# Contiguous 16-row partitions, the inverse second stage and the skip inside the MLP loop, streamed constants, table halves in a pipeline, LayerNorm on two engines

## The chip, the cores and the metric

The kernel runs on one core of one Trainium2 chip. The metric is the device time of one execution in microseconds (us); lower is better. A time without more words is the median of several executions, with their lowest and highest value in brackets. The engines are PE (TensorE, matmul; PEld is its weight load), DVE (VectorE), ACT (ScalarE), POOL (GpSimd) and SP (the queue that issues the DMAs). Tiles whose names begin with `ps_`, `pk` or `ml_p` hold what PE wrote (PSUM); to evacuate one is to copy it out with ACT or DVE. The granted clock (PEclk) is the share of full speed that PE was given.

## The reference

One state-space layer (the kernel K is a sum over 128 complex exponentials per channel, applied by FFT as a long convolution), then a gated MLP, both behind a LayerNorm and with a residual. L is 2048, D is 640, N is 128, F is 1728, all in bf16.

```python
# cut: input generation, dtype helpers
def _A_ref(u, A_re, A_im, B_re, B_im, C_re, C_im, log_dt, Dskip):
    dt = jnp.exp(log_dt)[:, None]
    logdA = dt * A                                        # A, Bc, Cc complex, D x N
    P = jnp.exp(logdA[:, :, None] * l[None, None, :])      # l = 0..2047, as bf16
    K = jnp.einsum("dn,dnl,dn->dl", Cc, P, dt * Bc).real
    # ... Kf, Uf = rfft of K and u padded to 2 L
    y = irfft(Uf * Kf)[..., :L]
    return y + u * Dskip

def _B_ref(x, w_gate, w_up, w_down):
    return (sigmoid(x @ w_gate) * (x @ w_up)) @ w_down

h   = A_u + _A_ref(layernorm(A_u), ...)
out = h + _B_ref(layernorm(h), w_gate, w_up, w_down)
```

## The kernel before

The FFT is done as two stages of small DFT matmuls. The kernel K is made as a product of two tables of powers, A and B, that DVE builds by complex multiplications; 160 matmuls per half of the channels ("kernel matrix", `pk`) multiply them. `kv` is the diagonal part of that product in the layout that the spectrum needs. The channels are worked in two halves of 320, because the tables of one half fill the memory for tables. The parts that matter, in program order:

```python
def kmm(hf, kw):                                  # kernel matrix of one half
    for g0 in range(0, G, 6):
        # 12 matmuls into pk[:, i, :], then a strided cast on ACT
        nc.scalar.copy(kts[:, :, g0:g0 + n].rearrange("p x g -> p g x"), pk[:, 0:n, :])
    for m in range(4):
        for c in range(4):                        # 16 small DMAs move the diagonals
            sy.dma_start(kv[32*m:32*m+32, :, c*G:c*G+G], kts[c::4, 4*m+c:4*m+c+65:16, :])
    # ... and 5 for klast
def kspec(hf, kv, xu, ...):                       # spectrum of one half, 9 pairs
    for qp in range(9):
        # per q: load mk, 10 matmuls ps_xk, ACT: xk<-ps_xk
        # DVE: t1 = xu*xk, t2 = xu*swap(xk)
        # PE: inverse first stage ps_g from t1, t2;  ACT: g_stg<-ps_g;  DMA to d
        # ... cut
def is2(hf, g2, h, sd):                           # inverse second stage and skip, 16 rows
    for r in range(16):
        # us loaded from ud (u * Dskip, stored earlier); identity matmul of us
        # 4 matmuls of 32 columns with W4; DVE: h = ps_y + h
        # ... cut

# order
# LayerNorm statistics of 16 rows on DVE, bases, apply
u_s1()                                            # first stage -> d1u in DRAM
nc.vector.tensor_tensor(u[:], u[:], dsk, ALU.mult); sy.dma_start(ud[:], u[:])
chain_a(0); chain_b(0)                            # tables of half 0, DVE
u_s2(xu, W2, a2p)                                 # second stage, both halves
kv = kmm(0, kw)
bases(1); chain_a(1)
kspec(0, kv, ...)
chain_b(1)
kv = kmm(1, kw)
kspec(1, kv, ...)
is2(0, ...); is2(1, ...)
mlp(...)       # 4 row groups; LayerNorm of the next group after feature tile 6
# ... cut: allocations, constants, weight loads
```

Of the kernel before, what the change touches and what calls it, by code (L numbers as in the profile page):

```python
# [14 lines left out]
P = 128  # L15
D = 640
NSLOT = 72
# [8 lines left out]
A_STEPS = [(slice(3, 4), slice(1, 2), 2), (slice(5, 8), slice(1, 4), 4), (slice(9, 13), slice(1, 5), 8), (slice(13, 16), slice(5, 8), 8),  # L26
           (slice(17, 22), slice(1, 6), 16), (slice(22, 27), slice(6, 11), 16), (slice(27, 32), slice(11, 16), 16)]
# [3 lines left out]
NTS = 5  # L31


def host_consts():
    p = np.arange(128)
    j1 = p & 31
    F1 = np.zeros((128, 64))
    for col in range(64):
        F1[:, col] = np.cos(2 * np.pi * j1 * col / 64) if col < 33 else -np.sin(2 * np.pi * j1 * (col - 32) / 64)
    ri, j2 = p >> 6, p & 63  # L40
    k1 = np.arange(33)[:, None]
    k2 = np.arange(64)[None, :]
    phi = 2 * np.pi * j2[:, None, None] * (k1 + 64 * k2)[None] / 4096
    W2re = np.where(ri[:, None, None] == 0, np.cos(phi), np.sin(phi))
    W2im = np.where(ri[:, None, None] == 0, -np.sin(phi), np.cos(phi))
    q = np.arange(17)[None, :, None]
    l2 = np.arange(64)[None, None, :]
    psi = 2 * np.pi * l2 * (2 * q + ri[:, None, None] + 64 * j2[:, None, None]) / 4096
    W3a = np.concatenate([np.cos(psi), np.sin(psi)], axis=2)
    W3b = np.concatenate([-np.sin(psi), np.cos(psi)], axis=2)  # L50
    row = p & 63
    k1r = np.where(row < 33, row, row - 32)
    w = np.where((row == 0) | (row == 32), 1.0, 2.0)
    l1 = np.arange(32)[None, :]
    W4b = np.where(row[:, None] < 33, np.cos(2 * np.pi * k1r[:, None] * l1 / 64), -np.sin(2 * np.pi * k1r[:, None] * l1 / 64)) * w[:, None] / 4096
    W4 = np.zeros((128, 2, 32))
    for hh in range(2):
        W4[64 * hh:64 * hh + 64, hh] = W4b[64 * hh:64 * hh + 64]
    sel = np.zeros((128, 4, 32))
    for i in range(4):  # L60
        sel[0:i + 1, i, 31] = 1.0
    lr = np.arange(2048).astype(np.float32).astype(ml_dtypes.bfloat16).astype(np.int64)
    f = np.arange(34)[:, None] + 64 * np.arange(64)[None, :]
    E = np.exp(-2j * np.pi * (np.arange(2048)[:, None] * f.reshape(1, -1) % 4096) / 4096)
    S = np.zeros((2049, f.size), np.complex128)
    np.add.at(S, lr, E)
    S = S.reshape(2049, 34, 64)
    S[:, 33] = 0
    M = np.zeros((17, 128, 2, 5, 128))
    a = np.arange(32)  # L70
    for m in range(4):
        for j in range(5):
            blk = S[B_VAL[4 * j + m] + 8 * a]
            blk = blk.reshape(32, 17, 128).transpose(1, 0, 2)
            M[:, 32 * m:32 * m + 32, 0, j] = blk.real
            M[:, 32 * m:32 * m + 32, 1, j] = blk.imag
    return {"ident": np.eye(128), "F1": F1, "W2": np.stack([W2re, W2im], axis=1).reshape(128, -1),
            "W3": np.stack([W3a, -W3a, W3b], axis=1).reshape(128, -1), "W4": W4.reshape(128, -1), "sel": sel.reshape(128, -1),
            "M": M.reshape(17, 128, 1280)}


def Lview(dram2d):
    return dram2d.rearrange("(l1 q r) d -> q l1 r d", l1=32, q=4, r=16)
# [21 lines left out]
def full_kernel(tc, ins, out):  # L105
# [5 lines left out]
    xv, ov = Lview(x2d), Lview(o2d)  # L111
# [3 lines left out]
    d1u = dram.tile([64, NSLOT, D], BF16, name="d1u")  # L115
    ud = dram.tile([P, 16, D], BF16, name="ud")
    d2 = [dram.tile([64, 64, w], BF16, name=f"d2_{i}") for i, (_, w) in enumerate(HALVES)]
# [5 lines left out]
    stp = sc.pool("s1stg", bufs=3)  # L123
# [18 lines left out]
    for rg in range(4):  # L142
        for q in range(4):
            sy.dma_start(u[32 * q:32 * q + 32, 4 * rg:4 * rg + 4, :], xv[q][:, 4 * rg:4 * rg + 4, :])
# [4 lines left out]
    dsk = early.tile([P, D], BF16, name="dsk")  # L149
    sy.dma_start(dsk[:], ins["A_Dskip"].rearrange("(o d) -> o d", o=1).to_broadcast((P, D)))  # L150
    F1 = cload(cp, "F1", [P, 64])
    W4 = cload(cp, "W4", [P, 2, 32])
    sel = cload(cp, "sel", [P, 4, 32])
# [19 lines left out]
    phi = par.tile([P, D], I32, name="phi")  # L173
    nc.vector.tensor_scalar(phi[:], rr[:], 2.0 ** 32, None, ALU.mult)
# [6 lines left out]

    mv = early.tile([P, 16, 2], F32, name="mv")
    rstd = early.tile([P, 16], F32, name="rstd")
    nmr = early.tile([P, 16], F32, name="nmr")
    st = early.tile([P, 16, 2, 6], F32, name="ln_st")

    def ln_stats(st, mv, src, r):
        for hh in range(2):
            nc.vector.bn_stats(st[:, r, hh, :], src[:, r, 320 * hh:320 * hh + 320])  # L189
        nc.vector.bn_aggr(mv[:, r, :], st[:, r, :, :].rearrange("p a b -> p (a b)"))  # L190

# [6 lines left out]
    mhalf = cp.tile([P, 16], F32, name="mhalf")  # L198
    nc.gpsimd.memset(mhalf[:], -0.5)

    def ln_apply(dst, src, r, c):
        nc.vector.tensor_scalar(dst, src, rstd[:, c:c + 1], nmr[:, c:c + 1], ALU.mult, ALU.add)  # L202

    for r in range(16):
        ln_stats(st, mv, u, r)


    CB = par.tile([P, 2, D], BF16, name="CB")
# [12 lines left out]
    g.tensor_tensor(CB[:, 0, :], c1[:], c2[:], ALU.subtract)  # L221
    g.tensor_tensor(cr[:], cr[:], dbi[:], ALU.mult)
    g.tensor_tensor(ci[:], ci[:], dbr[:], ALU.mult)
    g.tensor_tensor(CB[:, 1, :], cr[:], ci[:], ALU.add)
# [6 lines left out]

    def base_group(hf, ks, i0):
        o, w = HALVES[hf]
        n = len(ks)
        ph = btmp.tile([P, 3, WM], I32, name="b_ph")
        for i, k in enumerate(ks):
            if k:
                nc.vector.tensor_single_scalar(ph[:, i, 0:w], phi[:, o:o + w], k, ALU.logical_shift_left)
            else:
                nc.vector.tensor_copy(ph[:, i, 0:w], phi[:, o:o + w])  # L240
        ab = btmp.tile([P, 3, WM], F32, name="b_ab")
        nc.scalar.activation(ab[:, 0:n, 0:w], ph[:, 0:n, 0:w], AF.Abs)
        sn = btmp.tile([P, 3, WM], BF16, name="b_sn")
        nc.scalar.activation(sn[:, 0:n, 0:w], ph[:, 0:n, 0:w], AF.Sin, scale=SIN_SCALE)
        cs = btmp.tile([P, 3, WM], BF16, name="b_cs")
        nc.scalar.activation(cs[:, 0:n, 0:w], ab[:, 0:n, 0:w], AF.Sin, scale=-SIN_SCALE, bias=hpi[:, 0:1])
        return sn, cs
# [4 lines left out]
    def open_tables(hf):  # L252
# [3 lines left out]
        T["M"] = tabp.tile([P, 2, 6, w], BF16, name="tabM")  # L256

    def bases(hf):
        o, w = HALVES[hf]
        A, B, M, e = T["A"], T["B"], T["M"], E[hf]  # L260
        nc.gpsimd.memset(A[:, 0, 0, :], 1.0)
        nc.gpsimd.memset(A[:, 1, 0, :], 0.0)
        for gi, (i0, n) in enumerate(((0, 3), (3, 2), (5, 3), (8, 3))):
            ks = exps[i0:i0 + n]
            sn, cs = base_group(hf, ks, i0)
            if i0 < 5:
                for i in range(n):
                    j = A_BASE[i0 + i][0]
                    nc.vector.tensor_tensor(A[:, 0, j, :], e[:, i0 + i, :], cs[:, i, 0:w], ALU.mult)  # L269
                    nc.vector.scalar_tensor_tensor(A[:, 1, j, :], e[:, i0 + i, :], -1.0, sn[:, i, 0:w], ALU.mult, ALU.mult)  # L270
            else:
                m0 = i0 - 5
                nc.vector.tensor_tensor(M[:, 0, m0:m0 + n, :], e[:, i0:i0 + n, :], cs[:, 0:n, 0:w], ALU.mult)
                nc.vector.tensor_tensor(M[:, 1, m0:m0 + n, :], e[:, i0:i0 + n, :], sn[:, 0:n, 0:w], ALU.mult)
        nc.vector.tensor_copy(B[:, :, 0, :], CB[:, :, o:o + w])

# [10 lines left out]
    def chain_a(hf):  # L287
        for dst, src, mi in A_STEPS:
            cmul(T["A"], dst, src, T["A"], mi, HALVES[hf][1])

    def chain_b(hf):
        for dst, src, mi in B_STEPS:
            cmul(T["B"], dst, src, T["M"], mi, HALVES[hf][1])


    def u_s1():
        k = 0
        for lp in range(8):
            stg = stp.tile([P, 4, D], BF16, name="s1_stg")
            for (o, w) in HALVES:  # L300
                for qp in range(2):
                    ps = ps2.tile([P, 2, 512], F32, name="ps_s1", tag="p2")
                    for c in range(2):
                        for qi in range(2):
                            q = 2 * qp + qi
                            nc.tensor.matmul(ps[64 * c:64 * c + 64, qi, 0:w], lhsT=F1[32 * q:32 * q + 32, :],  # L306
                                             rhs=u[32 * q:32 * q + 32, 2 * lp + c, o:o + w], start=True, stop=True,
                                             tile_position=(32 * q, 64 * c))
                    nc.scalar.copy(stg[:, 2 * qp:2 * qp + 2, o:o + w], ps[:, :, 0:w])
            for c in range(2):  # L310
                j0 = 2 * lp + c
                rows = d1u[j0:j0 + 49:16, :, :]
# [316 lines left out]
```

## Time and profile before

626.74 us in three runs at first (625.21 to 627.21), 625.98 (622.04 to 627.21) with the fourth. The profiled execution has a span of 623.8 us.

| engine | busy us | share of span |
|---|---|---|
| PE | 408.8 | 66% |
| DVE | 278.8 | 45% |
| ACT | 218.8 | 35% |

No engine bounds the whole. First, the page of the kernel before, its part 2: each digit is the busy share, in tenths, of one of 40 slices (15.6 us each).

```profile
...
PE   1000520347781367899345567386999999999997
...
DVE  5797999300009998420012123757622322332331
...
DMA  9500522597301144431269996934001001001001
...
```

PE is little used in the first eight slices (125 us) while DVE is full for most of them, PE is full at the end (the last 12 digits, the MLP), and in between the engines take turns. The turns are read from windows. This is the busy time of each engine in stretches of the kernel before; the columns are named in the second line, and a number in brackets is a count of instructions.

```profile
...
core 0: us, PE busy (x) PEld busy (x) DVE busy (x) ACT busy (x) POOL busy (x), PEclk, DMA share, GB/s
76.00:114.00 38.00, 10.51 (x76) 5.51 (x75) 35.64 (x50) 13.22 (x20) 0.00 (x0) 1.00 0.27 73
114.00:131.00 17.00, 0.06 (x1) 0.00 (x0) 2.90 (x1) 0.00 (x0) 0.63 (x1) 1.00 0.77 278
...
317.00:387.00 70.00, 46.35 (x303) 26.23 (x303) 14.20 (x28) 22.23 (x33) 0.00 (x0) 0.85 0.89 241
428.00:619.00 191.00, 190.99 (x1074) 91.81 (x1073) 63.51 (x114) 38.81 (x64) 3.77 (x6) 1.00 0.06 15
...
```

DVE works 35.64 of the 38 us before 114; then everything waits while data travel (PE 0.06 of 17 us); the spectrum of half 1 takes 70 us for 46.35 us of PE at a DMA share of 0.89; the MLP is PE alone, at a granted clock of 1.00.

The waits between are in the PE timeline of the kernel before. The columns are start, duration, what ran, and in brackets how long PE had been idle and for what it waited.

```profile
...
63.88 0.83 PE L306 MATMUL ps_s_351<-u,c_F_114 32*64 32x320 bf16 x4 [37.54 <-DVE u L202]
...
109.25 1.70 PE L360 MATMUL pk<-tabB,tabA 128*128 128x84 bf16 x9 [14.21 <-DVE tabB L284]
110.88 0.48 PE L306 MATMUL ps_s_572<-u,c_F_114 32*64 32x320 bf16 x4
111.29 2.77 PE L360 MATMUL pk<-tabB,tabA 128*128 128x84 bf16 x15
131.49 0.45 PE L340 MATMUL ps_s_671<-a2g,c_W_665 128*64 128x320 bf16 x1 [17.44 <-DMA a2g<-d1u]
...
199.94 5.11 PE L385 MATMUL ps_xk<-kv,mk 128*128 128x320 bf16 x20 [14.39 <-DMA klast_d<-kts]
...
317.05 3.36 PE L385 MATMUL ps_xk<-kv,mk 128*128 128x320 bf16 x12 [14.39 <-DMA klast_d<-kts]
```

The first-stage matmuls start at 63.9 us. At 109 us the tables of half 0 are done and 24 matmuls of the kernel matrix run; the trace has them ahead of the second stage, although the text of the program has them after it. The last four matmuls of the first stage (`ps_s_572`) stand behind nine of them and so come only at 110.9 us, 16 us after the four before them (94.56). Then PE stands before the second stage and waits 17.44 us for the first stage's data to come back from DRAM. That is not transit alone: the skip product, which waits for these four (DVE, 111.4 us, 5.49 us long), its store (issued at 116.9) and the load of W2 (124.6) come first, and the first loads of a2g are issued from 125.1 on. Twice, ahead of each half's spectrum, PE waits 14.39 us for the small transfers of kv and klast.

### The profile page before, as it was taken

How to read it: one execution, taken by the hardware profiler on the slowest of the kernel's cores; microseconds unless marked ns; L12 is line 12 of the kernel's file. 1: busy time of each engine (PE TensorE's matmuls, PEld its weight loads, DVE VectorE, ACT ScalarE, POOL GpSimd, SP SyncE). 2: the span in 40 equal slices, each digit the busy share in tenths (PEclk: the TensorE clock that was granted, in tenths of full speed). 3: DMA queues.
4: the chain of work that ended last, by engine and by line, in shares of the span. 5: the costliest groups of instructions: out<-in, count | busy, mean ns of one | idle time of the engine just before them, and what ended most of it. 6: DMA issues, size and time to landing. Idle time of an engine off the chain costs nothing.

```text
span 623.8 us, 6408 instructions
## 1 busy us (share of the span) xinstructions
PE 408.8 (66%) x2470; PEld 223.2 (36%) x2470; DVE 278.8 (45%) x492; ACT 218.8 (35%) x280; POOL 25.3 (4%) x30
## 2 busy tenths in 40 slices
PE   1000520347781367899345567386999999999997
PEld 1000100224671134667323344123444444444443
DVE  5797999300009998420012123757622322332331
ACT  5630661048994033477522333002311310310210
POOL 0342000000000000000000000002000000000000
PEclk9999999995655687786577888757999999999999
DMA  9500522597301144431269996934001001001001
GB/s 184 138 0 0 164 56 76 211 243 163 108 1 28 42 123 114 115 89 46 57 141 243 245 296 183 203 82 142 1 2 42 1 1 42 1 1 42 2 1 42
DMA packets 44638, 57.26 MB, mean 92 GB/s; under 512 B 13496, under 2 KB 37568, under 8 KB 43840
## 3 DMA queue, kind: packets, MB, share of 16 engines
q1 hardware_dynamic: 44608, 56.86, 34.6%
q8 instruction: 19, 0.31, 0.2%
q14 instruction: 11, 0.09, 0.0%
HBM read 40.29 MB, written 15.73 MB: 90 GB/s over the span
## 4 chain that ended last, share of the span: by engine, by line
PE 40%; DMA 4%; DVE 2%; SPq 2%; issue 1%; ACT 1%; POOL 0%; DVEq 0%; POOLq 0%
PE ml_po L562 10%; PE ml_pg L550 10%; PE ml_pu L550 10%; PE ps_xk L385 5%; DMA us<-ud 3%; SPq L365 2%; PE ps_g L401 1%; PE ps_y L421 1%; PE ps_y L424 1%; DMA mk<-s4c_M 1%; ACT xk L386 1%; PE ml_pt L537 1%; DVE ln_2779 L533 0%; PE ps_y L427 0%; DVE ln_st L189 0%
## 5 line engine op out<-in xcount | busy, mean ns | idle before, releaser
L385 PE MATMUL ps_xk<-kv,mk 128*128 128x320 bf16 x340 | 66.0, 362 | 37.3 <-DMA klast_d<-kts 28.8
L552 ACT ACTIVATE ml_sg<-ml_pg 128x512 bf16<-128x512 f32 (+1 forms) x56 | 33.4, 597 | 130.6 <-PE ml_pg L550 129.1
L360 PE MATMUL pk<-tabB,tabA 128*128 128x84 bf16 x320 | 58.5, 352 | 21.8 <-DVE tabB L284 15.8
L550 PE MATMUL ml_pu<-lnT,Wu 128*128 128x512 bf16 (+1 forms) x280 | 70.8, 381 | 0.0
L553 DVE TENSOR_TENSOR ml_hm<-ml_pu,ml_sg 128x512 bf16<-128x512 f32 (+1 forms) x56 | 38.6, 690 | 70.7 <-PE ml_pu L550 67.8
L550 PE MATMUL ml_pg<-lnT,Wg 128*128 128x512 bf16 (+1 forms) x280 | 69.6, 380 | 0.0
L562 PE MATMUL ml_po<-Wd,ml_hm 128*128 128x512 bf16 x448 | 64.5, 300 | 0.0
L385 PEld LDWEIGHTS <-mk 128*128 128x128 bf16 x340 | 37.8, 116 | 65.8 <-DMA klast_d<-kts 29.4
L361 ACT CAST kts<-pk 128x504 bf16<-128x504 f32 (+1 forms) x28 | 59.3, 2236 | 6.0 <-PE pk L360 5.5
L360 PEld LDWEIGHTS <-tabA 128*128 128x128 bf16 x320 | 50.9, 161 | 28.6 <-issue 25.1
L386 ACT CAST xk<-ps_xk 128x640 bf16<-128x640 f32 x34 | 23.5, 693 | 62.2 <-PE ps_xk L385 37.5
L562 PEld LDWEIGHTS <-ml_hm 128*128 128x128 bf16 x448 | 33.1, 97 | 31.7 <-issue 9.0
L550 PEld LDWEIGHTS <-Wg 128*128 128x128 bf16 (+1 forms) x280 | 27.1, 99 | 33.3 <-issue 2.8
L405 ACT CAST g_stg<-ps_g 128x640 bf16<-128x640 f32 (+1 forms) x34 | 22.5, 689 | 47.1 <-PE ps_g L401 38.7
L550 PEld LDWEIGHTS <-Wu 128*128 128x128 bf16 (+1 forms) x280 | 27.4, 99 | 31.3 <-issue 0.3
L564 DVE TENSOR_TENSOR ml_out<-ml_po,h 128x640 bf16<-128x640 f32 x16 | 13.2, 825 | 51.3 <-PE ml_po L562 51.3
L401 PEld LDWEIGHTS <-c_W_906 64*128 64x128 bf16 x264 | 16.0, 107 | 50.0 <-issue 45.3
L269 DVE TENSOR_TENSOR tabA<-e_146,b_cs 128x320 bf16<-128x320 bf16 x5 | 1.5, 322 | 68.9 <-PE pk L360 68.8
L306 PEld LDWEIGHTS <-c_F_114 32*64 32x64 bf16 x128 | 4.5, 123 | 64.6 <-issue 64.6
L306 PE MATMUL ps_s_351<-u,c_F_114 32*64 32x320 bf16 x4 | 0.8, 444 | 37.5 <-DVE u L202 37.5
L340 PEld LDWEIGHTS <-c_W_665 128*64 128x64 bf16 x132 | 10.7, 145 | 31.6 <-issue 26.8
L428 DVE TENSOR_TENSOR h<-ps_y,h 128x320 bf16<-128x320 f32 x32 | 15.6, 491 | 12.2 <-PE ps_y L424 7.5
(303 smaller groups left out, 482.7 us busy)
## 6 DMA issues: line engine op xcount, KB each, us to landing
mk<-s4c_M SPq DMA_DIRECT2D x34, 320.0 KB, 3.5
d1u<-s_stg SPq DMA_DIRECT2D x32, 160.0 KB, 2.6
a2g<-d1u SPq DMA_DIRECT2D x15, 320.0 KB, 6.1
u<-in_A_u_dram SPq DMA_DIRECT2D x16, 160.0 KB, 6.1
ud<-u SPq DMA_DIRECT2D x1, 2560.0 KB
h<-in_A_u_dram SPq DMA_DIRECT2D x4, 640.0 KB, 7.3
g_0_1957<-d_0_59 SPq DMA_DIRECT2D x2, 1280.0 KB
us<-ud SPq DMA_DIRECT2D x16, 160.0 KB, 3.4
```

Source lines behind the costliest of these rows:

```text
L360: nc.tensor.matmul(pk[:, i, :], lhsT=Av[ri][:, :, g0 + i], rhs=Bv[ri][:, :, g0 + i], start=(ri == 0), stop=(ri == 1))
L361: nc.scalar.copy(kts[:, :, g0:g0 + n].rearrange("p x g -> p g x"), pk[:, 0:n, :])
L385: nc.tensor.matmul(ps[:, ri, 0:w], lhsT=mk[:, ri, j, :], rhs=kv[:, j, :], start=(j == 0), stop=(j == 4))
L386: nc.scalar.copy(xk[:, qi, :, :], ps[:, :, 0:w])
L401: nc.tensor.matmul(ps[:, kpar, 0:w], lhsT=W3[sl, wi, q, :], rhs=t[sl, qi, ro, :], start=(i == 0), stop=(i == 3), tile_position=(64 * kpar, 0))
L405: nc.scalar.copy(stg[:, 2 * (q % 2):2 * (q % 2) + nk, :], ps[:, 0:nk, 0:w])
L428: nc.vector.tensor_tensor(h[:, r, o:o + w], ps[:, 0, 0:w], h[:, r, o:o + w], ALU.add)
L550: nc.tensor.matmul(ps[0:fw, :], lhsT=W[:, dc, f0:f0 + fw], rhs=rhs, start=(dc == 0), stop=(dc == 4))
L552: nc.scalar.activation(sg[0:fw, :], pg[0:fw, :], AF.Sigmoid)
L553: nc.vector.tensor_tensor(hm[0:fw, ft, :], pu[0:fw, :], sg[0:fw, :], ALU.mult)
L562: nc.tensor.matmul(po[:, c0:c0 + w], lhsT=hm[0:fw, ft, 128 * lr:128 * lr + 128], rhs=Wd[0:fw, ft, c0:c0 + w], start=(ft == 0), stop=(ft == ...
L564: nc.vector.tensor_tensor(ob[:, lr, :], po[:], h[:, l2r, :], ALU.add)
```

## The change

The intent: put 16 consecutive rows on a partition (longer contiguous transfers, full 128-row DFT matmuls, half the inverse matmuls); work the second stage by halves, so that half 0's runs beside the table chain; stream W2 and W3 in groups instead of keeping them; take kv out with matmuls (`pick`) instead of small DMAs; run the spectrum as a software pipeline, one pair behind; do the statistics of 8 of 16 rows on ACT; and do the inverse second stage and the skip of 12 of the 16 rows inside the MLP's loop. The diff, cut to its core:

```diff
-    for r in range(16):
+    for r in range(NDV):                              # 8 rows on DVE, 8 on ACT
         ln_stats(st, mv, u, r)
...
-        for m in range(4):
-            for c in range(4):
-                sy.dma_start(kv[32 * m:32 * m + 32, :, ...], kts[c::4, 4 * m + c:4 * m + c + 65:16, :])
+                for m in range(4):
+                    nc.tensor.matmul(pv, lhsT=pick[:, c, m, :], rhs=kts[:, 4 * m + c:4 * m + c + 65:16, :], ...)
+                nc.scalar.copy(kvv[:, :, c, g1:g1 + GC], pv)
...
+        prev = None
+        for qp in range(9):
+            cur = front(qp)                           # mk matmuls, xk, products
+            if prev is not None:
+                back(*prev)                           # inverse matmuls of the pair before
+            prev = cur
+        back(*prev)
...
-    nc.vector.tensor_tensor(u[:], u[:], bc(dsk[:, None, :], (P, 16, D)), ALU.mult)
-    sy.dma_start(ud[:], u[:])
     chain_a(0)
-    chain_b(0)
-    u_s2(xu, W2, a2p)
-    kv = kmm(0, kw)
-    bases(1)
+    bases(1, "A")
+    u_s2(0, xu, a2p, nc.scalar.copy)
+    chain_b(0)
+    bases(1, "B")
+    kv = kmm(0, ktp, kx)
+    u_s2(1, xu, a2p, nc.vector.tensor_copy)
+    seeds(1)
     chain_a(1)
...
-    is2(0, g2[0], h, sd)
-    is2(1, g2[1], h, sd)
...
-            if rc < 3 and ft == 6:
-                prep(rc + 1)
+            if rc < 3 and ft == 4:
+                prep(rc + 1, nxt)                     # now with the inverse stage of 4 rows
+                if rc < 2:
+                    nxt = tail_loads(rc + 2)          # loads h and g2, makes the skip product
# ... cut: layouts, constants, allocations
```

## The prediction

> **What bounds it now.** No single engine: PE is busy 66% of 623.8 us, DVE 45%, ACT 35%. Timeline and per-window busy times give a chain of stages:
> - 0-114: DVE, almost without pause (36 of 38 us in 76-114). LN stats are spread through the table chains, so first-stage matmuls start only at 63.9. GpSimd makes it worse: while it works at 25-38 us a 128x320 DVE op takes 1.65 us instead of 0.32. The Trainium skill ("GPSIMD Engine Reference", Specifications) says the two share SBUF interfaces; the trace agrees.
> - 114-157: PE waits 17.4 us for the round trip of the first-stage spectrum, then the second stage at DMA pace (227 GB/s, DMA share 1.02).
> - 157-203: kmm half 0 (30 us; strided ACT cast 2.24 us, PE 0.18 us a matmul), then 14.4 us of PE idle while small kv DMAs are issued.
> - 203-317: half 1's tables (DVE) beside spectrum of half 0, kmm half 1, 14.4 us idle for kv again.
> - 317-387: spectrum half 1, 70 us for 46 us of PE: DMA share 0.89, mk waits, and a 1.64 us PE wait for DVE per pair.
> - 387-429: inverse second stage, 11 us PE idle for skip data; LN.
> - 429-620: MLP, PE 190 of 191 us at clock 1.0.
>
> **What the change does, costed.**
> 1. Half of LN stats (8 x 0.95 us) leave DVE for ACT; against it half 1's bases come early (4 us). Summing DVE durations in the new order: chain B(0) ends at about 102 (was 109), first stage at about 80 (was 112), so second stage of half 0 runs beside chain B. kmm(0) starts about 104 instead of 157: the largest gain.
> 2. kv by pick matmuls: removes 14.4 us idle twice, adds 80 small matmuls per half (7-13 us, estimate from 0.1-0.19 us each). kmm about 43 us: ends 147 (was 203).
> 3. Second stage of half 1 comes after, evacuated by DVE (17 x 0.74 us): 16 us given back. Then DVE must do both chains of half 1 plus products, 72 us by sum from 147. kmm(1) starts about 229, ends about 272 (kv ready was 317).
> 4. Spectrum half 1: PE work falls (half the inverse matmuls, software pipelining) to 34 us, but mk, W3, weights and stores are about 12.8 MB; at 250 GB/s about 50 us, DMA-bound. Ends about 322 (was 387).
> 5. Only four rows' inverse stage stays before the MLP, which starts about 347 (was 429): g_1 round trip, then rows 4-7's h and g2 loads queue behind Wd and block in-order DVE and PE.
> 6. MLP grows: 12 rows x 6 matmuls (10 us), and three DVE bursts of about 13 us (PSUM adds, stats, LN, skip) against 9-10 us of PE work behind them: 8 us of stalls. MLP 210 us (was 191).
>
> Sum: 347 + 210 + 4, plus 2 for profile against timing: **563 us**, range 537 to 590. Faster 0.97, same 0.02, slower 0.01.
>
> **What would show it.** Windows: first kmm matmul near 104, first spectrum product near 175, first spectrum-1 matmul near 272 without kv DMA wait; DMA share over 0.9 in spectrum half 1; first gate matmul near 347; three PE gaps of 2-4 us near ps_y in the MLP; 1.6 us DVE ops during GpSimd work still there.
>
> **What would make it wrong.** 640-byte runs of the split a2g loads slower than 5 KB runs; PE clock staying low (0.53 in kmm before), making kmm and spectrum PE-bound; spectrum half 1 less DMA-bound (upside 12 us); bursts stalling the MLP more, or the MLP losing its clock of 1.0, which alone would cost tens of us.

## The result, and the profile after

557.17 us (556.89 to 558.31, 4 runs) against 625.98. The ratio is 0.8914, 95% interval 0.8871 to 0.8957. A ratio is the mean time of one kernel's fast runs over that of the other's of the same rounds, so it is not quite the ratio of the medians. Executions over 1.5% slower than the fastest of the same kernel are left out of the means. The changed kernel is faster by about 11%.

The page of the changed kernel, part 2 (40 slices of 13.9 us), lines that answer to those of before and the clock:

```profile
...
PE   1201734789655885699968359799979999999997
...
DVE  4899899400589999200653275732273236322321
...
PEclk9999998555557898555799669799988999999999
DMA  7330546500253477001798991200100010001001
...
```

DVE is now full for most of the first half. The exception is the kernel matrix of half 0: from 114.2 to 143.2 us DVE is busy for 1.6 of 29 us, since the tables of half 1 take the memory of half 0's, which are still being read; ACT (26.5 us busy) and PE (26.8 us, at a granted clock of 0.50) set the pace there. The MLP (the last 16 digits of PE) is no longer all nines in its clock. Busy time in stretches of the changed kernel, columns as before:

```profile
...
100.00:146.00 46.00, 40.89 (x260) 32.88 (x260) 6.95 (x26) 41.75 (x46) 0.67 (x2) 0.50 0.12 32
...
266.00:309.00 43.00, 34.02 (x236) 20.25 (x235) 23.42 (x45) 20.31 (x32) 0.00 (x0) 0.92 0.88 277
334.00:552.00 218.00, 207.81 (x1125) 99.97 (x1146) 86.65 (x163) 38.70 (x64) 3.94 (x6) 0.97 0.06 20
...
```

The first is the kernel matrix of half 0, the second the spectrum of half 1, the last the MLP, which became longer: 217.5 us from its first up matmul to the end of its last down matmul, against 191.2 before. Lines of the PE timeline of the changed kernel up to the MLP:

```profile
...
85.62 0.74 PE L352 MATMUL ps_s_562<-a2g,W2g 128*64 128x320 bf16 x4 [7.93 <-DMA a2g<-d1u]
...
100.30 1.71 PE L377 MATMUL pk<-tabB,tabA 128*128 128x84 bf16 x9 [0.43 <-DVE tabB L312]
...
```

```profile
...
225.78 3.59 PE L377 MATMUL pk<-tabB,tabA 128*128 128x84 bf16 x20 [5.92 <-DVE tabB L312]
...
301.45 2.89 PE L417 MATMUL ps_xk<-kv,mk 128*128 128x320 bf16 x20 [2.36 <-DMA mk<-s4c_M]
...
320.18 1.23 PE L474 MATMUL ps_y<-g_1_2551,c_W_101 128*128 128x320 bf16 x4 [6.11 <-DMA g_1_2551<-d_1_59]
...
334.32 0.56 PE L605 MATMUL ml_pu<-lnT,Wu 128*128 128x512 bf16 x1 [0.22 <-issue]
...
```

The kernel matrix of half 0 starts at 100.3 us, amid the second stage. No wait for klast is left. The spectrum of half 1 waits for mk. Then the last result of half 1 goes to DRAM and back (6.11 us of PE) and the MLP starts at 334.3. Inside the MLP there are new gaps:

```profile
...
350.19 2.88 PE L619 MATMUL ml_po<-Wd,ml_hm 128*128 128x512 bf16 x19
355.59 1.46 PE L590 MATMUL ml_pt<-c_ident,ln_2845 128*128 128x128 bf16 x8 [2.52 <-DVE ln_2845 L586]
...
359.53 4.62 PE L605 MATMUL ml_pg<-lnT,Wg 128*128 128x512 bf16 x15
...
365.07 1.24 PE L605 MATMUL ml_pg<-lnT,Wg 128*128 128x512 bf16 x5
...
```

PE waits 2.52 us for DVE's LayerNorm, the eight transposes after it take 1.46 us, and then 15 gate matmuls take 4.62 us, where groups of 5 take 1.24 us a little later.

Where the time went, from the two traces (us from the start):

| point | before | after | gained so far |
|---|---|---|---|
| first matmul of kernel matrix, half 0 | 109.3 | 100.3 | 9 |
| kernel matrix, half 0, done (last cast) | 187.9 | 146.1 | 42 |
| kernel matrix, half 1, starts | 255.0 | 225.8 | 29 |
| spectrum of half 1 starts | 317.1 | 266.1 | 51 |
| spectrum of half 1 ends | 386 | 309 | 77 |
| first up matmul of the MLP | 428.1 | 334.3 | 94 |
| end | 623.8 | 555.7 | 68 |

The gain isn't steady: 13 us of it are lost between the first two kernel matrices, and 26 us in the MLP. The experiments look for what each part of the change is worth, above all of the parts where the gain shrinks.

### The profile page after: what moved, and what is told of

Same layout as the page of the kernel before. It is cut to its first block, busy times and chain, and to the rows that moved or that the text cites. A ratio compares the mean times of both kernels' runs of the same rounds, so it can differ in the third digit from the quotient of the medians.

```text
span 555.7 us, 6282 instructions
## 1 busy us (share of the span) xinstructions
PE 412.9 (74%) x2417; PEld 233.8 (42%) x2440; DVE 294.1 (53%) x518; ACT 234.1 (42%) x341; POOL 26.4 (5%) x35
## 4 chain that ended last, share of the span: by engine, by line
PE 49%; DVE 27%; ACT 9%; DMA 9%; issue 2%; POOL 2%; SPq 1%; POOLq 0%; DVEq 0%; ACTq 0%
PE ml_pg L605 11%; PE ml_po L619 10%; PE ml_pu L605 10%; PE pk L377 7%; DVE tS L310 5%; ACT kts L378 5%; PE ps_xk L417 4%; DMA mk<-s4c_M 4%; DVE ln_st L216 3%; DVE tabB L311 3%; DVE u L235 2%; PE ps_kv L385 2%; DMA W2g<-s4c_W 2%; DVE tabB L312 2%; DVE h L478 2%
## 5 line engine op out<-in xcount | busy, mean ns | idle before, releaser
L378 ACT CAST kts<-pk 128x420 bf16<-128x420 f32 x32 | 62.8, 2081 | 9.8 <-PE pk L377 9.3
L619 PE MATMUL ml_po<-Wd,ml_hm 128*128 128x512 bf16 (+3 forms) x438 | 64.8, 298 | 0.6 <-issue 0.2
L417 PE MATMUL ps_xk<-kv,mk 128*128 128x320 bf16 x340 | 57.2, 328 | 10.0 <-DMA mk<-s4c_M 8.9
L389 DVE TENSOR_TENSOR klast<-ps_kv,uhead 4x20 bf16<-4x20 f32 x32 | 4.8, 166 | 65.4 <-ACT kv L387 65.4
L591 ACT COPY lnT<-ml_pt 128x512 bf16<-128x512 bf16 x8 | 4.7, 586 | 61.6 <-PE ml_pt L590 61.6
L332 PEld LDWEIGHTS <-c_F_99 128*128 128x128 bf16 x64 | 8.0, 126 | 51.7 <-issue 47.5
L449 ACT CAST g_stg<-ps_g 128x640 bf16<-128x640 f32 x32 | 21.0, 699 | 10.1 <-PE ps_g L445 7.5
L352 PEld LDWEIGHTS <-W2g 128*64 128x64 bf16 x136 | 10.0, 156 | 33.4 <-DMA W2g<-s4c_W 20.1
L478 DVE TENSOR_TENSOR h<-ps_y,h 128x640 bf16<-128x640 f32 x16 | 12.8, 819 | 13.9 <-PE ps_y L474 12.7
L310 DVE TENSOR_TENSOR tS<-tabA,tabMA 128x3200 bf16<-128x3200 bf16 (+3 forms) x14 | 19.5, 1393 | 0.7 <-ACT tabA L302 0.4
```

Of the source, the lines that this page charges most:

```text
L310: nc.vector.tensor_tensor(t, X[:, :, src, :], mm, ALU.mult)
L417: nc.tensor.matmul(ps[:, ri, 0:w], lhsT=mk[:, ri, j, :], rhs=kv[:, j, :], start=(j == 0), stop=(j == 4))
L449: nc.scalar.copy(stg[0][:, 2 * (q % 2):2 * (q % 2) + 2, :], ps[:, :, 0:w])
L478: nc.vector.tensor_tensor(hv, ps[:, :, 0:w], hv, ALU.add)
L619: nc.tensor.matmul(po[:, c0:c0 + w], lhsT=hm[0:fw, ft, 128 * lr:128 * lr + 128], rhs=Wd[0:fw, ft, c0:c0 + w], start=(ft == 0), stop=(ft == ...
```

## The experiments

Names with e change one thing in the changed kernel, names with b one thing in the kernel before, and c are combinations. Each ran with runs of the kernel before on its chip. The ratio to compare with is 0.8914 for experiments e and c, and 1 for b. The intervals of the ratios are half to three quarters of a per cent to each side, so where a difference is smaller than one per cent the times alone don't settle it, and the trace's points are given as well. All kernels gave correct results.

### b3: order alone, in the kernel before

```diff
-    u_s2(xu, W2, a2p)
-    kv = kmm(0, kw)
+    kts = kmm(0, kw)
+    u_s2(xu, W2, a2p)
+    kv = kvmove(0, kts, kw)      # the small DMAs of kv
```

> The kernel before with one change of order: the 160 kernel-matrix matmuls of half 0 come ahead of the second stage on PE, and the small kv transfers come after it; nothing else of the change. Theory (order alone gives most of the gain: PE waited 17.4 us for the spectrum's round trip while the tables were ready, and the tables of half 1 wait for half 0's kernel matrix to free their buffers): kernel matrix of half 0 from about 114 to 146, second stage to about 168, the table chain of half 1 and with it kernel matrix of half 1 start 30 to 40 us earlier (about 215 to 225 instead of 255), total 586 to 597 against 623 to 627. Rival (PE and DMA do the same work in series whatever the order; only the 17 us of waiting are filled): total 606 to 612.

Measured: 607.11 us (605.92 to 608.77) against 624.95, ratio 0.9718 (0.9679 to 0.9758). From the PE timeline of b3:

```profile
...
127.28 4.35 PE L360 MATMUL pk<-tabB,tabA 128*128 128x84 bf16 x24 [14.03 <-ACT kts L361]
...
195.60 4.26 PE L390 MATMUL ps_xk<-kv,mk 128*128 128x320 bf16 x20 [13.99 <-DMA mk<-s4c_M]
...
```

And from its ACT timeline:

```profile
...
124.97 8.95 ACT L361 CAST kts<-pk 128x504 bf16<-128x504 f32 x4 [13.68 <-DMA ud<-u]
...
```

The rival's number came true, but not its reason. The kernel matrix of half 0 runs from 108.5 to 153 us with a wait of 14.03 us in it: the first cast into kts waits 13.68 us until the store of the skip (`ud<-u`) has landed, since kts lies in the memory that u leaves. The second stage takes until 181, the kv transfers aren't hidden (13.99 us before 195.6), and the spectrum of half 0 starts 4 us earlier than before; the theory, with the second stage over at about 168, had it some 30 us earlier. The kernel matrix of half 1 starts at 219 instead of 255, as the theory had it, but with half 0's spectrum unfinished; the two share PE until 282, where before it was done at 302. So this order alone gives 18 of the 68 us. With the skip's store gone as well it should give more; that pair was not run and is left open.

### b1: the skip made again instead of stored and loaded, in the kernel before

```diff
-    nc.vector.tensor_tensor(u[:], u[:], bc(dsk...), ALU.mult)
-    sy.dma_start(ud[:], u[:])
 # in is2
-                sy.dma_start(us[:], ud[:, r:r + 2, o:o + w])
+                for i in range(2):
+                    nc.vector.tensor_scalar(us[:, i, :], h[:, r + i, o:o + w], rstd..., nmr..., ALU.mult, ALU.add)
+                    nc.vector.tensor_tensor(us[:, i, :], us[:, i, :], dsk[:, o:o + w], ALU.mult)
```

> The kernel before with the skip product made again from h in the inverse stage instead of stored after the first stage and loaded again. Theory (the skip's store stands ahead of the second stage's loads in the queue and its product ahead of them on DVE, and the inverse stage waits 11 us for its reload): second stage starts about 119 instead of 131.5, the inverse stage of half 0 has no 11 us wait, total 18 to 26 us less (600 to 607). Rival (the DVE product and store are hidden behind the spectrum's own store and load, and the recomputation, 64 DVE operations of 0.2 to 0.3 us, paces the inverse stage instead): less than 10 us gained, 614 to 624.

Measured: 619.79 us (616.31 to 623.84) against 624.95, ratio 0.9922 (0.9864 to 0.9979). From the PE timeline of b1, ahead of the second stage and in the inverse stage:

```profile
...
125.10 5.14 PE L340 MATMUL ps_s<-a2g,c_W 128*64 128x320 bf16 x32 [11.46 <-DMA a2g<-d1u]
```

```profile
...
410.80 0.45 PE L423 MATMUL ps_y<-us,c_ident 128*128 128x320 bf16 x1 [0.83 <-DVE us L421]
...
```

The rival held. The wait for the spectrum's round trip is 11.46 us instead of 17.44, so the skip's product and store had cost 6 us, not 12; the rest is the round trip itself. Those 6 to 8 us stay up to the end of half 1's spectrum, and then DVE, which makes the skip row by row, paces the inverse stage. The first up matmul of the MLP is at 428.6, where before it was at 428.1. The profiled run was also the slowest of the four, so how much of the 0.8% is real is open.

### e1: LayerNorm statistics back on DVE

```diff
-    ln_stats_act(slice(NDV, 16))
+    for r in range(NDV, 16):
+        ln_stats(st, mv, u, r)
```

> The changed kernel with the LayerNorm statistics of rows 8 to 15 put back on DVE (8 times 0.95 us as the trace of before has it). Theory (DVE paces the stretch to kmm half 0): the chain of tables of half 0 ends 7 to 8 us later (108 instead of 100.5 us), first kmm matmul near 108, total 563 to 565 us against 557.2. Rival (the statistics on ACT delay ACT's evacuation of the first stage by as much as they spare DVE): chain and total within 2 us of the changed kernel, 555 to 559.

Measured: 556.34 us (555.53 to 559.01), ratio 0.8947 (0.8883 to 0.9012): not told apart from the changed kernel. My theory fell. The PE timeline of e1:

```profile
...
91.32 1.28 PE L352 MATMUL ps_s<-a2g,W2g 128*64 128x320 bf16 x8 [1.40 <-DMA W2g<-s4c_W]
103.24 3.57 PE L377 MATMUL pk<-tabB,tabA 128*128 128x84 bf16 x20 [10.64 <-DVE tabB L312]
...
```

The table chain of half 0 ends only 2.9 us later (103.2 against 100.3), and the second stage of half 0 is over at 92.6 instead of 106.4: without the statistics ACT evacuates the first stage sooner, so the second stage begins at 74.0 instead of 85.6. So the rival's total came true, and in part its reason. The kernel matrix then runs without second-stage matmuls between, and its last matmul starts at 139.9 in both traces. Why only 2.9 us and not 7.6? The DVE timeline of the changed kernel shows what the statistics made room for:

```profile
...
23.59 8.75 DVE L235 TENSOR_SCALAR u<-u,rstd,nmr 128x640 bf16<-128x640 bf16 x8
...
63.13 2.94 DVE L235 TENSOR_SCALAR u<-u,rstd,nmr 128x640 bf16<-128x640 bf16 x8
...
```

Eight LayerNorm applies take 8.75 us beside GpSimd's work, and 2.94 us after it. In e1 the statistics stand there instead, at 0.42 us for half a row as elsewhere, and the applies come later, at 0.37 us. This agrees with the Trainium skill, "GPSIMD Engine Reference", Specifications, which says that GpSimd's contention is with DVE instructions in a 2-port mode or with two SBUF inputs: the applies were slowed here and the statistics not, and a product with two inputs in SBUF that ran beside GpSimd in e1 took 1.05 and 1.75 us instead of 0.65. Whether the applies use the 2-port mode no run here shows.

### e4: no GpSimd in the early part

```diff
-    g = nc.gpsimd
+    g = nc.vector            # C and B products; f_*, c1, c2 in bf16 instead of fp32
```

> The changed kernel with the C and B products of the early part done by DVE in bf16, nothing by GpSimd there. Theory (GpSimd slows DVE while it works): a 128x320 DVE op that took 1.65 us beside GpSimd takes 0.3 to 0.4 us, the first u apply x8 falls from 8.75 to about 3 us, DVE gets about 3.4 us of products to do, the chain of half 0 ends about 5 us earlier (95 to 97 instead of 100.5) and the total is 551 to 554. Rival (those long ops wait on something else, such as loads, or the early part is paced by loads of h): ops as long as before or idle in their place, total 556 to 561.

Measured: 552.24 us (550.36 to 556.92), ratio 0.8879 (0.8814 to 0.8943). From the DVE timeline of e4:

```profile
...
24.40 2.58 DVE L235 TENSOR_SCALAR u<-u,rstd,nmr 128x640 bf16<-128x640 bf16 x7
...
```

The applies take 2.58 us for seven. The first matmul of the kernel matrix is at 94.3 instead of 100.3, that of half 0's spectrum at 159.5 instead of 165.0, and the first up matmul of the MLP at 328.9 instead of 334.3. The theory held: a shift of 5 to 6 us went through undiminished from the first stage to the MLP. By the times alone the difference is within the intervals.

### e3: kv by DMA as before

```diff
-        # pick and last matmuls, kv<-ps_kv on ACT, 4 groups of 20
+        for m in range(4):
+            for c in range(4):
+                sy.dma_start(kv[m::4, :, c * G:c * G + G], kts[c::4, 4 * m + c:4 * m + c + 65:16, :])
+        # ... klast by 5 DMAs, as before
```

> The changed kernel with kv and klast taken out of kts by small DMAs as in the kernel before, no pick matmuls. Theory (the pick matmuls cost on PE nearly what they save in idle time: 43 us for the kernel matrix with them, 30 to 34 without, against 14.4 us of waiting for kv): half 0's transfers hide behind the second stage of half 1, and half 1 waits 14 us after a kernel matrix 9 us shorter; total 551 to 560 against 557. Rival (the transfers wait behind other transfers and cost the full 14 us twice, as before): total 566 to 576.

Measured: 550.31 us (549.71 to 551.21), ratio 0.8812 (0.8773 to 0.8852): 7 us less than the changed kernel, a little better than the theory's range. PE waits in e3:

```profile
...
154.18 1.28 PE L352 MATMUL ps_s<-a2g,W2g 128*64 128x320 bf16 x8 [14.61 <-DMA W2g<-s4c_W]
...
257.62 6.40 PE L400 MATMUL ps_xk<-kv,mk 128*128 128x320 bf16 x30 [14.04 <-DMA klast_d<-kts]
...
```

The kernel matrix of half 1 takes 212.4 to 243.5, 31 us, where it took 40 with the pick matmuls, and then PE waits 14.04 us: 5 us lost. In half 0 the transfers also cost a wait, 14.61 us of PE in front of the second stage (the loads of W2g stand behind them in the queue), but PE isn't what half 0 waits for; DVE is, and its chain of half 1 begins as soon as the product is done (and, as c1 below shows, some of its casts move into time when it is idle). The kernel matrix of half 1 starts 13.4 us earlier (212.4 against 225.8). So taking kv out with matmuls lost about 7 us: it removed idle time of an engine that had time, and put work ahead of the engine that had none.

### e8: the second stage of half 1 evacuated by ACT

```diff
-    u_s2(1, xu, a2p, nc.vector.tensor_copy)
+    u_s2(1, xu, a2p, nc.scalar.copy)
```

> The changed kernel with the second stage of half 1 taken out of PSUM by ACT instead of DVE (ACT was idle for 19.8 us there, from 147 to 168 us). Theory (from 147 to 226 us DVE paces the kernel: the table chains of half 1 wait behind 16 casts of 0.74 to 0.82 us): the chain of half 1 ends 10 to 12 us earlier (about 215 instead of 226) and the total is 544 to 548 against 557. Rival (that stretch is paced by its DMA, W2g waits of 8 us, and DVE's casts fit into waits that it had anyway): less than 3 us gained, 553 to 558.

Measured: 542.45 us (541.86 to 543.12), ratio 0.8721 (0.8653 to 0.8789). The DVE timeline of the changed kernel in that stretch, and ACT's:

```profile
...
149.97 0.81 DVE L354 CAST xu_551<-ps_s_1114 128x640 bf16<-128x640 f32 x1
150.70 1.15 DVE L310 TENSOR_TENSOR tS<-tabA,tabMA 128x1920 bf16<-128x1920 bf16 x1
...
```

```profile
...
167.73 0.69 ACT L418 CAST xk<-ps_xk 128x640 bf16<-128x640 f32 x1 [19.76 <-PE ps_xk L417]
...
```

DVE does 17 casts of about 0.8 us between the multiplications of the table chain, while ACT is idle for 19.76 us. With ACT doing the casts the kernel matrix of half 1 starts at 211.6 instead of 225.8 and the MLP at 317.3 instead of 334.3. The theory held, with 2 us more than it said. Of the losses tested ahead of the MLP this is the largest.

### e2: four mk buffers

```diff
-    mkp = sc.pool("mk", bufs=3)
+    mkp = sc.pool("mk", bufs=4)
+    w3p = sc.pool("w3", bufs=3)   # W3g in a pool of its own
```

> The changed kernel with four buffers instead of three for the mk tiles of the spectrum (W3g keeps three, in a pool of its own). Theory of bandwidth (the second half's spectrum runs at the pace of its DMA): spectrum of half 1 stays at 43 us, the mk waits (8.9 us in sum) only move, total within 1.5 us of 557.2. Rival (too few loads under way: latency): mk waits fall to 4 us or less, spectrum of half 1 becomes 38 to 40 us, total 552 to 554.

Measured: 551.01 us (549.27 to 552.33), ratio 0.8846 (0.8793 to 0.8899). The waits from the start of half 1's spectrum to its end, in the changed kernel and then in e2 (who waited, for whom, us in total, times, longest):

```profile
...
PEld L417 <- DMA mk<-s4c_M: 8.5, 5, 3.0
...
```

```profile
...
PEld L417 <- DMA mk<-s4c_M: 1.4, 2, 0.9
...
```

PE's wait for mk is gone (0.8 us in the whole run, 8.9 before), the last mk matmul starts at 299.8 instead of 306.3, and data move at 299 instead of 279 GB/s from 266 to 310 us. The MLP starts 4.0 us earlier. The theory of bandwidth fell: a DMA share of 0.88 was not a limit. It was mostly the number of loads under way.

### e7: half 1's spectrum in plain order

```diff
         for qp in range(9):
             cur = front(qp)
+            if hf == 1:
+                back(*cur)
+                continue
             if prev is not None:
                 back(*prev)
```

> The changed kernel with the spectrum of half 1 in plain order: each pair's inverse matmuls directly after its own mk matmuls, as the kernel before has them, not one pair later. Theory (the software pipeline is what took the 1.64 us wait for DVE per pair out and shortened the half's spectrum from 70 to 43 us): PE waits for ACT and DVE 1.5 to 2.5 us per pair, spectrum of half 1 takes 54 to 60 us, total 567 to 574. Rival (the transfers set the pace, so the wait for DVE replaces the waits for mk): spectrum 43 to 48 us, total 556 to 562.

Measured: 569.41 us (566.28 to 571.11), ratio 0.9147 (0.9079 to 0.9214). From the PE timeline of e7:

```profile
...
286.92 0.89 PE L445 MATMUL ps_g<-t,W3g 64*128 64x320 bf16 x8 [2.87 <-DVE t L425]
...
```

PE waits 2.87 us for DVE in each pair, longer than the 1.64 us of the kernel before, because two additions on DVE were put between (they halve the inverse matmuls). The last mk matmul starts at 326.1 instead of 306.3. The theory held, with the half at about 63 us even longer than its 54 to 60: by the ratios the edit costs 14 to 15 us of the total. In the trace 18.5 us stand at the MLP's start and 9 us at its end; this execution was the fastest of the four, and its first row group took 48 us where the changed kernel's took 57. The trace shows why: in e7 the inverse stage of the second row group ran before the MLP (its last matmuls at 349 us), so that the transposes of that group follow at 363.8 with no gap and take 0.61 us for eight. The edit thus moved work out of the MLP as e6 does on purpose, and the 14 to 15 us are a net figure: about 20 us lost in the spectrum, some of it won back in the MLP.

### e5 and e6: the fold into the MLP

Two ways of undoing the bursts. e5 keeps the fold and spreads it over feature tiles; e6 puts the inverse stage of all rows ahead of the MLP.

```diff
# e5
-            if rc < 3 and ft == 4:
-                prep(rc + 1, nxt)
+            if rc < 3:
+                spread(rc + 1, nxt, ft)   # one row's inverse stage per tile 1-4, statistics 2-5,
+                                          # apply 7-8, transposes 10-11
# e6
+    for rc in (1, 2, 3):
+        is2(pso_p, "ml_po", rc, tail_loads(rc))   # before the loop; prep does LayerNorm only
```

> The changed kernel with the preparation of the next row group (inverse stage, LayerNorm, transposes) spread over the feature tiles 1 to 11 of the MLP instead of in one burst after tile 4. Theory (the burst makes PE wait for DVE, and after each gap the gate matmuls run at a lower clock: x15 in 4.5 us instead of 3.2): the gaps of 2.5, 2.3 and 1.0 us and the clock loss go, a row group with preparation takes 51 to 53 us instead of 57, the MLP 201 to 206 us instead of 217.5, total 541 to 546. Rival (the 10 us more of a row group is the added PE and DVE work itself): a row group stays at 55 to 57 us, total 554 to 558.

> The changed kernel with the inverse second stage and skip of all 16 rows ahead of the MLP, as the kernel before has it; LayerNorm, transposes and tail loads as changed. Theory (the fold into the MLP's loop costs there, 27 us more than the MLP of before, about what it saves ahead of it): the MLP starts 15 to 25 us later (350 to 360 instead of 334), takes 196 to 202 us instead of 217.5, total 549 to 564. Rival (folding hides the inverse stage nearly whole): the MLP is shortened by less than 8 us and the total is 567 to 580.

Measured: e5 541.04 us (539.36 to 545.26), ratio 0.8698 (0.8636 to 0.8760); e6 540.33 us (539.13 to 542.05), ratio 0.8650 (0.8613 to 0.8686). In e5 the transposes follow an up matmul with no gap and at full clock, and so do the gate matmuls after them:

```profile
...
358.14 0.61 PE L612 MATMUL ml_pt<-c_ident,ln 128*128 128x128 bf16 x8
...
359.67 1.24 PE L627 MATMUL ml_pg<-lnT,Wg 128*128 128x512 bf16 x4
...
```

The MLP stretches of e5 and of e6, as windows:

```profile
...
331.00:534.00 203.00, 200.70 (x1128) 98.20 (x1149) 87.13 (x164) 38.36 (x64) 3.79 (x6) 1.00 0.06 23
...
```

```profile
...
346.00:534.00 188.00, 184.89 (x1031) 88.98 (x1050) 69.07 (x132) 35.72 (x60) 3.78 (x6) 1.00 0.04 14
...
```

The granted clock is 1.00 in both, 0.97 in the changed kernel. In e5 PE is busy 200.70 of 203 us: the MLP takes about 15 us less than the 217.5. Nearly the same number of matmuls took 7.1 us less of busy time than in the changed kernel (200.70 against 207.81), and PE was idle for 2.3 us instead of 10.2. A row group takes 51 to 54 us instead of 56 to 57.5. In e6 the first up matmul of the MLP is at 332.7, not 350 to 360: until 347 us, when the whole inverse stage is over, its matmuls and those of the first row group alternate on PE. The first row group ends at 391.5, at the same time as in the changed kernel, which had done the inverse stage of 8 rows by then and not of 16. From there the groups take 47.8 us each. The theory for e5 held. For e6 both theories fell: the total was below both ranges, since, as the row groups' ends show, the inverse stage of the other rows cost nothing at the front. The fold into the loop, as written, cost about 16 us.

### c1 and c2: what helped, together

c1 has the edits of e2, e3, e4 and e6 (W3g has two buffers and is loaded after mk, as memory was short). c2 is c1 with the edit of e8.

```diff
# c1 -> c2
-    u_s2(1, xu, a2p, nc.vector.tensor_copy)
+    u_s2(1, xu, a2p, nc.scalar.copy)
```

> The changed kernel with what helped so far: four mk buffers (W3g two, loaded after mk), kv by small DMAs, the C and B products on DVE, the inverse stage of all rows ahead of the MLP. If the gains add (0.7, 1.0, 0.5 and 2.6 per cent by the ratios so far): 528 to 532. If they overlap (an earlier front only makes the transfers of the second half pace it): 535 to 541.

> The combined kernel of the run before, with the second stage of half 1 taken out of PSUM by ACT as well. If the gain adds to the others (12 to 15 us off the table chains of half 1, as measured alone): 508 to 512 against 522.7. Rival (in the combined kernel that stretch is held by the wait of 14.6 us for W2g behind the small kv transfers, so DVE's casts run in time that is lost anyway): 517 to 521.

Measured: c1 522.73 us (521.56 to 526.01), ratio 0.8410 (0.8348 to 0.8473); c2 519.40 us (518.04 to 521.95), ratio 0.8337 (0.8303 to 0.8371). c1's gains add within the noise: the product of the four ratios to the changed kernel, times 0.8914, is 0.845, inside c1's interval. In us it came out below both ranges that were expected. c2 gained 3 to 5 us and not 14; the rival's range held, but its reason only in part. The DVE timeline of c1, and that of c2:

```profile
...
103.81 2.29 DVE L354 CAST xu<-ps_s 128x640 bf16<-128x640 f32 x3 [2.13 <-PE ps_s L352]
...
135.07 0.48 DVE L310 TENSOR_TENSOR tS<-tabA,tabMA 128x640 bf16<-128x640 bf16 x1
...
```

```profile
...
138.40 0.49 DVE L310 TENSOR_TENSOR tS<-tabA,tabMA 128x640 bf16<-128x640 bf16 x1 [31.64 <-ACT tabA L302]
...
```

In c1, without the pick matmuls, DVE had already done nine of the 17 casts before its chain of half 1 began, in time when it was idle anyway (six during half 0's kernel matrix, three at its end, 132.9 us). In c2 ACT does them, between its casts of kts; its copies that begin the tables of half 1 come 3.3 us later, and DVE waits for them until 138.4 instead of beginning at 135.1. So ACT's help takes the other eight casts, about 6 us, off DVE's chain and gives 3 us back: the kernel matrix of half 1 starts at 203.1 instead of 206.9. c2 beats both kernels: 17% less than before, and about 6.5% less than the changed kernel (by the ratio of the two ratios).

## Why the prediction was right or wrong

The time was right: 563.0 us predicted, 557.2 measured, well inside 537 to 590. That the sum came so close is partly luck, since the two errors that matter were of opposite sign: the MLP started 13 us earlier than predicted and took 7.5 us longer.

1. **LN and tables of half 0.** Chain end about 102, measured 100.5; kernel matrix about 104, measured 100.3. The dates held. The cause that I gave did not: e1 shows that moving the statistics to ACT is worth nothing in the total, since the 8.75 us apply beside GpSimd took most of the room, and the second stage of half 0 ended 14 us later for it, as ACT was slower with the first. I put the gain down to the order (second stage beside the chain, LayerNorm applied early); that is argued, and e1 shows only that it was not the second engine.
2. **Pick matmuls.** 43 us for the kernel matrix, end 147; measured 45.8 us, end 146.1. I counted two removed waits of 14.4 us as gain. e3 shows that the exchange lost 7 us: half 0's wait fell on PE, while DVE set the pace.
3. **Second stage of half 1, DVE.** First product 175, kernel matrix of half 1 229; measured 177.6 and 225.8. Right, also in the cause: e8 took the casts off DVE and the start moved to 211.6.
4. **Spectrum of half 1.** This is the mis-sized term: "about 50 us, DMA-bound", measured 43 to 44. The bytes were right (12.27 MB by the trace, 12.8 predicted), the rate of 250 GB/s was not: 279 came, and 299 with one more buffer (e2). I had taken a high DMA share for a ceiling. What the pipeline does, I had as one term of PE work; without it, in e7, the spectrum took about 20 us longer, and the total, net of what the MLP won back, 14 us.
5. **MLP start.** 347 predicted, 334.3 measured; the distance from the end of the spectrum is 25 us in both. The content was wrong in part: no wait behind Wd was seen; PE waited 6.11 us for g_1 and then 5.70 us for DVE, which makes skip and LayerNorm.
6. **MLP.** 210 us predicted, 217.5 measured. The mis-sized term is what comes after a gap. The 10 us of inverse-stage matmuls and the gaps of about 8 us in sum (2.52 + 0.41 + 0.67 in the first burst, 2.9 and 1.7 in the others) came as predicted. But after the first two gaps (2.52 and 2.29 us) PE ran at a lower clock for 6 to 7 us: 0.50 from 355.6 to 361 us in the first burst, where 15 gate matmuls took 4.62 us and not about 3.2. In the third burst, with gaps of 1.0, 0.4 and 0.3 us, the matmuls kept their speed (eight transposes in 0.61 us). I had named the loss of clock under what could go wrong and put nothing into the sum. e5 shows both losses gone at once, 15 us together. The two windows give an estimate of the parts: PE idle 7.9 us less, and 7.1 us less of busy time for nearly the same matmuls. No run removes one without the other.

The claim that b3 tested, that the earlier kernel matrix was "the largest gain", is too simple. Order alone gave 18 us. The rest needed its neighbours: by-half second stage, pipelined spectrum, half the inverse matmuls. For by-half second stage and the inverse matmuls no experiment stands alone, so their shares stay open.

## What to carry to other kernels

When work is moved off the critical engine, look at which engine sets the pace in that stretch, and at that engine only: ACT's 19.76 us of idle time was worth 14 us, and PE's idle 14 us of half 0 nothing. Don't take a busy DMA queue for a full one before one more buffer has been tried. When work is folded into a loop that keeps one engine full, spread it so that this engine never waits: in this kernel a gap of 2.5 us cost more than itself, since the clock fell after it, while one of 1.0 us did not.

## What the Trainium skill lacked or had wrong

- "TensorE: Matmul & The Clock Gate", Part 1, table of the two states: the page names an idle window of about 3.4 us before the clock falls. In the MLP of the changed kernel a single gap of 2.52 us, after PE had been busy without a break, was followed by transposes at less than half speed (1.46 us for eight, 0.61 in e5) and slow gate matmuls (4.62 us for 15). The granted clock was 0.50 from 355.6 to 361 us, and the same came after a gap of 2.29 us; after one of 1.01 us it didn't fall. A gap shorter than the length in the table was enough here. (Further on the same part tells of a kernel that loses its clock to short idle times between groups of matmuls, without a length.)
- The same section says that sustained activity of about 3.4 us releases the clock. In the kernel matrix PE was busy 40.89 of 46 us with a granted clock of 0.50 throughout (31.45 of 34 us in c1, also 0.50). How much activity is enough for these 84-column matmuls, each with a weight load of 0.16 us, the page doesn't say, and no run here tells.
- "GPSIMD Engine Reference", Specifications: right on whom GpSimd disturbs (statistics not slowed, applies 3 times as long), but this section gives no size. Here it was 8.75 against 2.94 us for eight applies, and by e4's trace 5 to 6 us up to the MLP's start.
- "Advanced Engine Details and Errata", SBUF Cachelines: the page says that another cacheline per access costs performance, without a figure. ACT's cast with a stride took 2.08 us for 420 elements; a contiguous one took 0.69 us for 640. The two differ in shape too, so this is not a clean measurement of the stride.
- "DMA: Bandwidth & Descriptors", the table of where the fixed cost of a transfer goes (a fit for DMAs from GpSimd's queue), gives about 50 ns for the dispatch and calls descriptor generation small; it has no issue time for the SP queue. On the SP queue of the kernel before, the 16 issues of kv took 10.54 us one after the other, 0.66 us each, at 34 GB/s. That is most of the 12.2 to 14.8 us that PE waited at these places in the kernels that move kv by DMA. The line of the SP queue in the kernel before:

```profile
...
187.88 10.54 SPq L365 DMA_DIRECT2D kv<-kts  x16
...
```
